# Homes of a kernel's work tiles set by a list, and a hidden unit's six products in a new order

## The chip, the cores and the metric

The kernel runs on one core of a Trainium2 chip. The metric is device time in microseconds of one execution, median of three runs: 706.25 us before (706.14 to 706.48).

## The reference

Attention through 32 memory slots per head, followed by a two-layer network with ELU, all float32:

```
a      = softmax of phi over the sequence            # phi [8, 8, 576, 32]
k_m    = a^T k ;  v_m = a^T v                        # per image and head [32, 64]
attn   = softmax over slots of (q k_m^T / 8)         # [576, 32]
x      = attn v_m, heads side by side                # [4608, 512]
h      = x w_in                                      # w_in [512, 2048]
g      = h if h > 0 else exp(min(h, 0)) - 1
out    = g w_out                                     # w_out [2048, 512]
```

There are 8 images (b) of 8 heads and 576 tokens.

## The kernel before

**Algebra.** v_m and w_in are multiplied first: for each image and each quarter c of the 2,048 hidden channels, `vw` (L723, matmuls at L557) makes a tile vw of 256 rows (8 heads x 32 slots, as two halves of 128) by 512 channels. Then h of a block is the product of vw with the softmax probabilities A (256 slots by 288 tokens, a half image).

**Two parts.** Products of float32 are split: a value is a high part (rounded to the fp32r type) and a low part (the rest), and a product is high x high + low x high + high x low. ScalarE writes the high part (`vw_high` L735, `probs_high` L701 and L702, `elu_high` L826), VectorE the low one (`vw_low` L741, `probs_low` L716, `elu_low` L832).

**A unit.** `order` lists 256 units (image b, half hf, channel tile j of 128 channels). For each, `hidden` (L770 on, matmuls at L779) issues six matmuls of 128x288 into one PSUM tile psh: three passes by two halves g of the slots. Weights (the stationary operand) are 128 columns of the vw tile, the moving operand is a part of A. Then ScalarE and VectorE make ELU (L794, L795, L806, L814), and `project` (by way of `by_channels`, L840) issues six matmuls of 128x512 for the two whole tiles of 128 tokens: there the weights are columns of gp (the two parts of g) and the moving operand is a row block wout[j] of w_out (two parts). The 32 tokens that remain of each half are gathered in rest tiles and projected together for two images (48 matmuls of L840).

**Order of the work.** Nothing is scheduled automatically: a list written out by hand (`FIRST`) gives the order of all steps of the first images, then a plan with a place for each step goes on. Each engine takes its instructions in that order and waits on semaphores. Hidden units run one to two units ahead of their project. Image 0 and 1 have their own front part; later ones prepare attention within the units of the image before.

**Homes.** SBUF tiles come from two pools, `const` (ident, win0 to win3) and `work`. A tile with a tag takes the next of the tag's `bufs` buffers; tags lie behind one another in the order in which they are first asked for. Tag vw has three buffers (three of four c of an image), the fourth, c = 3 of image 2 on, has a home of its own (tag c3). A has four buffers, gp three. wout0 to wout7 have one home each, wout8 to 11 lie in tag late2, wout12 to 15 in tag late3. The vw tile's four parts (high and low, two halves) lie 2,048 bytes apart, A's four parts 1,152, gp's two parts 1,024, a wout's two parts 2,048. Worked out from the sizes in their order, the homes modulo 512 bytes are:

| tile | before | after |
|---|---|---|
| the three vw homes | 160, 160, 160 | 416, 0, 64 (vw0, vw1, vw2) |
| c3 | 416 | 448 |
| A (all four) | 288 | 416 |
| gp (all three) | 416 | 288 |
| wout0 | 288 | 288 |
| wout1 to wout7 | 416 | 320, 352, 384, 416, 448, 480, 0 |
| wout8 to 11 (late2) | 224 | 0 |
| wout12 to 15 (late3) | 416 | 448 |

The queries of image 0 (qh) lie in the output buffers (tag osb); four touches, small DMAs at the start on ScalarE's queue, have small tiles of their own.

Of the kernel before, what the change touches and what calls it, by code (L numbers as in the profile page):

```python
# [1 line left out]

# [6 lines left out]
F32 = mybir.dt.float32  # L9
# [7 lines left out]
P = 128  # L17
# [20 lines left out]

W_SCALE = 2.0**-112
PASSES = ((HI, HI), (LO, HI), (HI, LO))  # L40


def rows_of(c):
# [126 lines left out]
"""  # L170


@with_exitstack
def fused_kernel(ctx: ExitStack, tc: tile.TileContext, phiT, phi, phit, kv0, kvt, kv, q0, q1, w_in, w_out, out):

# [14 lines left out]
    dram = ctx.enter_context(tc.tile_pool(name="dram", bufs=2, space=bass.MemoryType.DRAM))  # L190

    ident = const.tile([P, P], F32, name="ident")
    const.tile([P, 8], F32, name="pad_ident")
    make_identity(nc, ident)

    win = [const.tile([P, NPAIR, CW], F32, name=f"win{c}") for c in range(NVC)]
# [3 lines left out]

    spare = [work.tile([P, 4 * CW], F32, name="spare", tag="vw", bufs=NVB) for _ in range(2)]
    SPARE = {"e0": 0, "e1": 512, "e2": 1024, "x0": 1536, "x1": 1664, "k0": 1792,
             "sc0": 2048, "sc1": 2624, "pr0": 3200, "pr1": 3264}

# [47 lines left out]


    def load_phi(b):
        t = work.tile([P, 2, S], F32, name="ph", bufs=1)
        if b == 0:
            for g in range(2):
                nc.sync.dma_start(t[:, g], phiT[b, :, g])  # L260
        else:
            nc.sync.dma_start(t, phiT[b])
        st[b]["ph"] = t
# [13 lines left out]
    def spread_max(b):  # L277

        s = st[b]
        d = dram.tile([P, 2], F32, name="nmd")  # L280
        nc.sync.dma_start(d, s["nm"])
        s["nmb"] = work.tile([P, P, 2], F32, name="nmb", bufs=1)
        nc.sync.dma_start(
            s["nmb"].rearrange("p x a -> p (x a)"),
            d.rearrange("x a -> (x a)").partition_broadcast(P),
        )
# [63 lines left out]

    def load_half_q(b, hf):
        if b == 0:
            t = work.tile([P, NPAIR, HALF], F32, name="qh", tag="osb", bufs=2)
        else:
            t = half_of_1(hf).rearrange("p (a n) -> p a n", a=NPAIR)
        t0 = hf * HALF
        nc.sync.dma_start(t, q0[b, :, hf])
        for u, (u0, u1) in enumerate(units(b)):
            if t0 <= u0 < t0 + HALF:
                st[b]["q"][u] = t[:, :, u0 - t0 : u1 - t0]  # L360
# [67 lines left out]
    def dec_high(k):  # L428

        i = tiles[k][1]  # L430
        late = dict(tag=f"late{i // 4}", bufs=4) if i >= 8 else dict(bufs=1)
        wout[i] = work.tile([P, 2, DM], F32R, name=f"wout{i}", **late)
        nc.scalar.copy(wout[i][:, HI, :], made(k).rearrange("p r n -> p (r n)"))

# [9 lines left out]
    def phi_max(b, g=None):  # L444
        s = st[b]
        if "nm" not in s:
            s["nm"] = work.tile([P, 2], F32, name="nm")
            s["sums"] = work.tile([P, 2], F32, name="sums")
        g = slice(0, 2) if g is None else slice(g, g + 1)
        eng = nc.gpsimd if b in max_on_pool else nc.vector  # L450
        eng.tensor_reduce(s["nm"][:, g], s["ph"][:, g], AX.X, ALU.max, negate=True)
# [8 lines left out]
    def slot_scale(b):  # L460
        s = st[b]
        sums = s["sums"]
        nc.vector.tensor_scalar(sums, sums, EPS, None, ALU.add)
        rinv = work.tile([P, 2], F32, name="rinv")
        nc.vector.reciprocal(rinv, sums)
        s["rinv"] = rinv

# [61 lines left out]
    def kv_copy(b, i=(0, 1)):  # L529
        s = st[b]  # L530
        if "kvm" not in s:
            s["kvm"] = work.tile([P, 2, P], F32, name="kvm", bufs=2)
        ps = s["ps"].pop(("kv", i))
        if b >= NB:
            nc.scalar.copy(s["kvm"][:, i[0] : i[-1] + 1], ps)
            return
        if 0 in i:
            keys = s["keys"]
            for a in range(2):
                r = slice(64 * a, 64 * a + 64)  # L540
                copy = nc.vector.tensor_copy if (b, a) in keys_on_dve else nc.scalar.copy
                copy(keys[r, :, a * M : (a + 1) * M], ps[r, 0].rearrange("p (j m) -> p j m", m=M))
        if 1 in i:
            nc.scalar.copy(s["kvm"][:, 1], ps[:, len(i) - 1])
# [64 lines left out]
        s["sc"][u] = sc.rearrange("p (n m) -> p n m", m=SQ)  # L609

    def softmax_max(b, u):
        mx = work.tile([P, 2 * HALF // SQ], F32, name="mx")
        if b < NB:
            for ps, g in zip(st[b]["ps"]["s", u], TOKENS):
                nc.vector.tensor_reduce(
                    mx[:, g], ps.rearrange("p (n m) -> p n m", m=SQ), AX.X, ALU.max
                )
        else:
            sc = st[b]["sc"][u]
            mx = mx[:, : sc.shape[1]]  # L620
            nc.vector.tensor_reduce(mx, sc, AX.X, ALU.max)
        st[b]["mx", u] = mx
# [25 lines left out]
    def softmax_sum(b, u):  # L648
        sc = st[b]["sc"][u]
        n = sc.shape[1]  # L650
        sm = work.tile([P, 2 * HALF // SQ], F32, name="sm")[:, :n]
        nc.vector.tensor_reduce(sm, sc, AX.X, ALU.add)
        nc.vector.tensor_scalar(sm, sm, EPS, None, ALU.add)
        rs = work.tile([P, 2 * HALF // SQ], F32, name="rs")[:, :n]
        nc.vector.reciprocal(rs, sm)
        st[b]["rs", u] = rs

# [39 lines left out]
    def probs_high(b, u):  # L697
        s = st[b]
        if b < NB:
            A = s["A"][u] = work.tile([P, 2, 2, HALF], F32R, name="A", bufs=4)  # L700
            nc.scalar.copy(A[:, HI, :, : NT * P], s["ps"]["p", u])  # L701
            nc.scalar.copy(A[:, HI, :, NT * P :], s["pr", u])  # L702
            return
        for hf, src, dst in probs_parts(b, u):
            if s["A"][hf] is None:
                s["A"][hf] = work.tile([P, 2, 2, HALF], F32R, name="A", bufs=4)
            nc.scalar.copy(s["A"][hf][:, HI, :, dst], s["pr", u][:, :, src])

    def probs_low(b, u):
# [19 lines left out]
    def vw_high(b, c, n0=0, n1=CW, parts=(0, 1)):  # L729
        s = st[b]  # L730
        if s["vw"][c] is None:
            home = dict(tag="c3", bufs=1) if b >= NB and c == NVC - 1 else dict(tag="vw", bufs=NVB)
            s["vw"][c] = work.tile([P, 2, 2, CW], F32R, name="vw", **home)
        for a in parts:
            nc.scalar.copy(s["vw"][c][:, HI, a, n0:n1], s["ps"]["vw", c, n0][a])  # L735

    def vw_low(b, c, n0=0, n1=CW, parts=(0, 1)):
        s = st[b]
        t = s["vw"][c]
        for a in parts:  # L740
            nc.vector.tensor_tensor(  # L741
                t[:, LO, a, n0:n1], s["ps"]["vw", c, n0][a], t[:, HI, a, n0:n1], ALU.subtract
            )

    blocks = [(0, 0, 4), (1, 0, 4), (0, 4, 8), (1, 4, 12), (0, 8, 16), (1, 12, 16)]
# [17 lines left out]
    def rest_of(b, j):  # L763

        p, i = b // 2, j // 8
        if (p, i) not in rests:
            rests[p, i] = work.tile([P, 8, P], F32, name="rest", bufs=2)
        return rests[p, i][:, j % 8, :]

    def hidden(it):  # L770
        b, hf, j = order[it]
        s = st[b]
        t = s["vw"][j // 4]
        c0 = (j % 4) * P
        ps = ps_h.tile([P, HALF], F32, name="psh")
        n = 0
        for x, y in PASSES:
            for g in range(2):
                nc.tensor.matmul(  # L779
                    ps,  # L780
                    t[:, x, g, c0 : c0 + P],
                    s["A"][hf][:, y, g, :],
                    start=(n == 0),
                    stop=(n == 5),
                )
                n += 1
        gs[it] = ps

    def elu_exp(it):
        ps = gs[it]
        gf = work.tile([P, HALF], F32, name="gf", bufs=5)
        nc.scalar.activation(gf, ps, AF.Relu, scale=-1.0)  # L794
        nc.scalar.activation(gf, gf, AF.Exp, scale=-1.0)  # L795
        gs[it] = gf, ps
# [25 lines left out]
        nc.gpsimd.tensor_copy(rest_of(b, j)[:, o : o + REST], gf[:, NT * P :])  # L822

    def elu_high(it):
        gp = work.tile([P, 2, NT * P], F32R, name="gp", bufs=3)
        nc.scalar.copy(gp[:, HI], gs[it][:, : NT * P])  # L826
        gs[it] = gs[it], gp

# [51 lines left out]

    def rest_high(p, i):
        gf = rests[p, i // 4][:, i % 4 * 2 : i % 4 * 2 + 2, :]
        gp = work.tile([P, 2, NT * P], F32R, name="gp", bufs=3)
        nc.scalar.copy(gp[:, HI], gf.rearrange("p j n -> p (j n)"))  # L884
        gs["rest", p, i] = gf, gp

# [21 lines left out]
                out[2 * p + n // 2, n % 2, NT * P :], t[n * REST : (n + 1) * REST, :]  # L908
            )

    tiny = work.tile([P, 1], F32, name="tiny", bufs=1)
    work.tile([P, 24], F32, name="pad_tiny", bufs=1)
    warm = ps_o.tile([P, P], F32, name="pso00")

    touched = {
# [5 lines left out]
        "out": w_out[0][:, :8],  # L921
    }

    def touch(x):
        rows = touched[x]
        n = 16 * list(touched).index(x)
        t = work.tile([P, 16], F32, name=f"touch{n}", bufs=1)
        if x in ("in", "out"):
            t, rows = t.bitcast(U32), rows.bitcast(U32)
        nc.scalar.dma_start(t, rows)  # L930
# [168 lines left out]
```

## Time and profile before

| what | value |
|---|---|
| median of three runs | 706.25 us |
| the profiled execution | 706.02 us |
| its span, first to last instruction | 704.2 us |
| TensorE matmuls, busy | 695.2 us, 99% of the span |
| VectorE, ScalarE, busy | 454.7 us, 455.8 us |
| GpSimd, busy | 69.2 us |
| DMA | 64.50 MB in 26,450 packets |

A matmul's busy time runs from its start to the end of its drain, so busy times of matmuls that follow one another overlap, and the mean of one is longer than the distance of two starts. That distance has to be read from starts in order of time. A row of the order in time merges neighbouring instructions of a line: its start, its length to the last one's end, and the count.

### The profile page before, as it was taken

The page shows a single profiled execution, that of the slowest core. Times are in us where ns is not written, and L with a number is a line of the kernel's source. Part 1 is how long each engine was busy: PE and PEld are TensorE (multiplying, and loading weights), DVE is VectorE, ACT ScalarE, POOL GpSimd, SP SyncE. Part 2 cuts the span into 40 slices and gives each one's busy share as a digit, 9 for nine tenths or more (in the row PEclk, how much of TensorE's full clock was granted, in tenths as well). Part 3 has the DMA queues.
Part 4 walks back from the last instruction along what each step waited for, and adds up shares of the span by engine and source line. Part 5 has one row for each costly group of instructions (what it writes and reads, how often), then busy time and mean ns, then how long its engine had stood idle before and what let it go on. Part 6 is the DMA issues. An engine that isn't in the chain of part 4 may idle for free.

```text
span 704.2 us, 13637 instructions
## 1 busy us (share of the span) xinstructions
PE 695.2 (99%) x5112; PEld 579.1 (82%) x5112; DVE 454.7 (65%) x1207; ACT 455.8 (65%) x1101; POOL 69.2 (10%) x117
## 2 busy tenths in 40 slices
PE   8999999999999999999999999999999999999997
PEld 7778787878878888888887888878888888788886
DVE  4989887976686459554864648764683636944442
ACT  3879988877457556575654746765574655756652
POOL 0332342123000200020000200010000010000000
PEclk9999999999999999999999999999999999999999
DMA  8982023351313400351003520243001430000001
GB/s 339 407 356 90 1 63 121 114 153 24 135 39 110 175 31 2 98 172 69 1 1 112 165 76 1 65 118 126 31 1 52 119 152 31 1 31 1 30 2 46
DMA packets 26450, 64.50 MB, mean 92 GB/s; under 512 B 3984, under 2 KB 8592, under 8 KB 26384
## 3 DMA queue, kind: packets, MB, share of 16 engines
q1 hardware_dynamic: 25712, 63.46, 26.4%
q8 instruction: 41, 0.67, 0.4%
q10 hardware_dynamic: 672, 0.16, 0.1%
q14 instruction: 25, 0.20, 0.1%
HBM read 54.17 MB, written 9.44 MB: 90 GB/s over the span
## 4 chain that ended last, share of the span: by engine, by line
PE 94%; DMA 4%; DVE 0%; ACT 0%; issue 0%; SPq 0%
PE pso L840 57%; PE psh L779 29%; PE psb L557 4%; PE psb L498 2%; PE pso L557 2%; DMA raw<-w_out 2%; DMA raw<-w_in 1%; DMA qh<-q 1%; DMA touch<-kv 0%; PE psb L526 0%; PE psb L570 0%; PE pso L570 0%; PE psh L673 0%; SPq L323 0%; DVE A L716 0%
## 5 line engine op out<-in xcount | busy, mean ns | idle before, releaser
L840 PE MATMUL pso<-wout,gp 128*128 128x512 f32 x1728 | 439.2, 394 | 0.0
L840 PEld LDWEIGHTS pso<-wout,gp 128*128 128x128 f32 x1728 | 310.1, 188 | 61.3 <-issue 2.1
L779 PEld LDWEIGHTS psh<-A,vw 128*128 128x128 f32 x1536 | 226.6, 188 | 33.4 <-issue 9.2
L779 PE MATMUL psh<-A,vw 128*128 128x288 f32 x1536 | 244.0, 296 | 0.6 <-ACT A L702 0.4
L794 ACT ACTIVATE gf<-psh 128x288 f32<-128x288 f32 x256 | 105.1, 411 | 101.3 <-PE psh L779 98.1
L806 DVE SCALAR_TENSOR_TENSOR gf<-gf,psh 128x256 f32<-128x256 f32 x192 | 80.7, 420 | 136.4 <-ACT gf L795 135.8
L826 ACT CAST gp<-gf 128x256 fp32r<-128x256 f32 x256 | 103.2, 404 | 78.5 <-DVE gf L806 66.7
L832 DVE TENSOR_TENSOR gp<-gf,gp 128x256 fp32r<-128x256 f32 x256 | 113.4, 446 | 50.7 <-ACT gp L826 49.9
L795 ACT ACTIVATE gf<-gf 128x288 f32<-128x288 f32 x256 | 113.9, 445 | 8.1
L299 POOL TENSOR_TENSOR e<-e,nmb 128x512 f32<-128x512 f32 x12 | 16.4, 1384 | 359.4 <-ACT gf L794 234.7
L803 DVE SCALAR_TENSOR_TENSOR gf<-gf,psh 128x288 f32<-128x288 f32 x64 | 28.5, 450 | 17.5 <-ACT gf L795 15.8
L814 DVE SCALAR_TENSOR_TENSOR rest<-gf,psh 128x32 f32<-128x32 f32 x192 | 34.6, 180 | 0.0
L741 DVE TENSOR_TENSOR vw<-psb,vw 128x512 fp32r<-128x512 f32 (+2 forms) x48 | 26.9, 583 | 4.4 <-ACT vw L735 4.4
L884 ACT CAST gp<-rest 128x256 fp32r<-128x256 f32 x32 | 12.6, 405 | 21.9 <-PE pso L840 21.9
L822 POOL COPY rest<-gf 128x32 f32<-128x32 f32 x64 | 18.7, 319 | 70.3 <-DVE gf L803 62.8
L889 DVE TENSOR_TENSOR gp<-rest,gp 128x256 fp32r<-128x256 f32 x32 | 12.9, 420 | 15.7 <-ACT gp L884 15.6
L735 ACT CAST vw<-psb 128x512 fp32r<-128x512 f32 (+2 forms) x48 | 22.5, 496 | 0.4 <-PE psb L557 0.4
L557 PE MATMUL psb<-win,kvm 64*32 64x512 f32 (+2 forms) x384 | 22.3, 521 | 0.0
L397 ACT ACTIVATE mag<-raw 128x512 uint32<-128x512 uint32 x30 | 20.0, 671 | 2.7 <-DVE win L419 1.4
L393 ACT ACTIVATE mag<-raw 128x512 f32<-128x512 f32 x30 | 19.7, 667 | 1.0 <-DMA raw<-w_in 0.8
L741 DVE TENSOR_TENSOR vw<-pso,vw 128x512 fp32r<-128x512 f32 (+1 forms) x28 | 17.2, 625 | 0.7 <-ACT vw L735 0.6
L937 PE MATMUL pso<-ident 128*128 128x128 f32 x84 | 13.4, 325 | 1.6 <-POOL ident masks.py:199 1.6
(134 smaller groups left out, 445.8 us busy)
## 6 DMA issues: line engine op xcount, KB each, us to landing
kvt<-kv SPq DMA_DIRECT2D x32, 512.0 KB, 7.3
raw<-w_in SPq DMA_DIRECT2D x15, 512.0 KB, 9.7
raw<-w_out SPq DMA_DIRECT2D x15, 512.0 KB, 8.8
out<-osb SPq DMA_DIRECT2D x14, 512.0 KB, 2.8
qt<-q SPq DMA_DIRECT2D x18, 384.0 KB, 3.8
ph<-phiT SPq DMA_DIRECT2D x7, 576.0 KB, 5.1
e<-phi SPq DMA_DIRECT2D x12, 256.0 KB, 5.1
kvt<-kvt SPq DMA_DIRECT2D x8, 256.0 KB, 7.9
```

The source lines that it names most:

```text
L557: nc.tensor.matmul(outs[a][32 * j : 32 * j + 32, :], lhs[r, 32 * j : 32 * j + 32], rhs[r, j], start=True, stop=True, tile_position=(64 * a ...
L735: nc.scalar.copy(s["vw"][c][:, HI, a, n0:n1], s["ps"]["vw", c, n0][a])
L741: nc.vector.tensor_tensor(t[:, LO, a, n0:n1], s["ps"]["vw", c, n0][a], t[:, HI, a, n0:n1], ALU.subtract)
L779: nc.tensor.matmul(ps, t[:, x, g, c0 : c0 + P], s["A"][hf][:, y, g, :], start=(n == 0), stop=(n == 5),)
L794: nc.scalar.activation(gf, ps, AF.Relu, scale=-1.0)
L795: nc.scalar.activation(gf, gf, AF.Exp, scale=-1.0)
L803: nc.vector.scalar_tensor_tensor(gf, gf, -1.0, ps, ALU.add, ALU.max)
L806: nc.vector.scalar_tensor_tensor(gf[:, :n], gf[:, :n], -1.0, ps[:, :n], ALU.add, ALU.max)
L814: nc.vector.scalar_tensor_tensor(rest_of(b, j)[:, o : o + REST], gf[:, n:], -1.0, ps[:, n:], ALU.add, ALU.max)
L826: nc.scalar.copy(gp[:, HI], gs[it][:, : NT * P])
L832: eng.tensor_tensor(gp[:, LO], gf[:, : NT * P], gp[:, HI], ALU.subtract)
L840: nc.tensor.matmul(ps, gp[:, y], wout[j][:, x, :], start=(first and n == 0), stop=(last and n == 2),)
```

## The change

All work tiles get their homes by a list, `LAYOUT`, that is asked for at the start in that order (with fillers of 32 and 64 bytes); tiles then name their tags. The tile vw has parts 2,176 bytes apart in the order high 0, high 1, low 1, low 0. The three vw homes are named one by one and taken in a cycle. From unit 8 on, `hidden` issues its six products in the order TURN: for half 0 low x high, high x high, high x low, then the same for half 1 (weights' part first); units 0 to 7 keep the order of before (PLAIN). The queries of image 0 take buffers of tag A, the touches lie in one buffer of tag gf. Instructions keep their counts and shapes.

```diff
+PIECE = {(HI, 0): 0, (HI, 1): 1, (LO, 1): 2, (LO, 0): 3}
+STEP = CW + 32
+TURN = ((LO, 0, HI), (HI, 0, HI), (HI, 0, LO), (LO, 1, HI), (HI, 1, HI), (HI, 1, LO))
+PLAIN = ((HI, 0, HI), (HI, 1, HI), (LO, 0, HI), (LO, 1, HI), (HI, 0, LO), (HI, 1, LO))
+def piece(t, x, a, n0, n1):
+    o = PIECE[x, a] * STEP
+    return t[:, o + n0 : o + n1]
+SMALL = [("tiny", 32, 1)] + [(t, 8, 2) for t in ("nm", "sums", "rinv")]
+SMALL += [(t, 72, 2) for t in ("mx", "sm", "rs")]
+LAYOUT = SMALL + [("A", 4608, 4), ("vw0", 8576, 1), ("gp", 2048, 3), ("wout0", 4096, 1)]
+for i in range(1, 8):
+    LAYOUT += [(None, 32, 1), (f"wout{i}", 4096, 1)]
+LAYOUT += [("vw1", 8576, 1), ("gf", 1152, 5), ("late2", 4096, 4), ("t4k", 4096, 6), ("osb", 4096, 2)]
+LAYOUT += [("t2k", 2048, 7), ("kvm", 1024, 2), (None, 64, 1), ("vw2", 8576, 1), ("c3", 9216, 1)]
+LAYOUT += [("late3", 4096, 4), ("rest", 4096, 2), ("nmb", 1024, 1), ("ph", 4608, 1)]
...
-    const.tile([P, 8], F32, name="pad_ident")
...
-    spare = [work.tile([P, 4 * CW], F32, name="spare", tag="vw", bufs=NVB) for _ in range(2)]
+    homes(work)
+    spare = [work.tile([P, 4 * CW], F32, name="spare", tag=f"vw{i}", bufs=1) for i in range(2)]
+    vw_homes = itertools.cycle(("vw2", "vw0", "vw1"))
...
-            t = work.tile([P, NPAIR, HALF], F32, name="qh", tag="osb", bufs=2)
+            t = work.tile([P, NPAIR, HALF], F32, name="qh", tag="A", bufs=4)
...
-            home = dict(tag="c3", bufs=1) if b >= NB and c == NVC - 1 else dict(tag="vw", bufs=NVB)
-            s["vw"][c] = work.tile([P, 2, 2, CW], F32R, name="vw", **home)
+            home = "c3" if b >= NB and c == NVC - 1 else next(vw_homes)
+            s["vw"][c] = work.tile([P, 4 * STEP - 32], F32R, name="vw", tag=home, bufs=1)
         for a in parts:
-            nc.scalar.copy(s["vw"][c][:, HI, a, n0:n1], s["ps"]["vw", c, n0][a])
+            nc.scalar.copy(piece(s["vw"][c], HI, a, n0, n1), s["ps"]["vw", c, n0][a])
...
-        n = 0
-        for x, y in PASSES:
-            for g in range(2):
-                nc.tensor.matmul(
-                    ps,
-                    t[:, x, g, c0 : c0 + P],
-                    s["A"][hf][:, y, g, :],
-                    start=(n == 0),
-                    stop=(n == 5),
-                )
-                n += 1
+        for n, (x, g, y) in enumerate(PLAIN if it < 8 else TURN):
+            nc.tensor.matmul(
+                ps, piece(t, x, g, c0, c0 + P), s["A"][hf][:, y, g, :], start=(n == 0), stop=(n == 5)
+            )
...
-    work.tile([P, 24], F32, name="pad_tiny", bufs=1)
...
-        t = work.tile([P, 16], F32, name=f"touch{n}", bufs=1)
+        if not spots:
+            spots.append(work.tile([P, HALF], F32, name="gf", tag="gf", bufs=5))
+        t = spots[0][:, n : n + 16]
```

## Rows read from the trace of the kernel before

**Rows 1.** The spans and the granted clock.
```profile
core 0: 704.2 us, clock 1.000
```
**Rows 2.** The page, busy us, share of the span and instructions.
```profile
PE 695.2 (99%) x5112; PEld 579.1 (82%) x5112; DVE 454.7 (65%) x1207; ACT 455.8 (65%) x1101; POOL 69.2 (10%) x117
```
**Rows 3.** Busy time by stretch: stretch, its length, then us and instructions by engine.
```profile
220.00:640.00 420.00, 420.00 (x3035) 350.40 (x3034) 256.47 (x742) 260.94 (x638) 18.38 (x20) 1.00 0.21 70
```
**Rows 4.** TensorE's waits: us in total, times, longest us.
```profile
PE pso L937 <- POOL ident masks.py:199: 1.6, 1, 1.6
PE psh L779 <- ACT A L702: 0.4, 1, 0.4
```
**Rows 5.** Groups of TensorE's matmuls by form: busy us, mean ns, idle before.
```profile
L840 PE MATMUL pso<-wout,gp 128*128 128x512 f32 x1728 | 439.2, 394 | 0.0
L779 PE MATMUL psh<-A,vw 128*128 128x288 f32 x1536 | 244.0, 296 | 0.6 <-ACT A L702 0.4
```
**Rows 6.** TensorE in order of time, 552 to 570: start us, length us, count.
```profile
552.25 0.95 PE L779 MATMUL psh<-A,vw 128*128 128x288 f32 x6
554.42 0.95 PE L779 MATMUL psh<-A,vw 128*128 128x288 f32 x6
...
558.77 0.95 PE L779 MATMUL psh<-A,vw 128*128 128x288 f32 x6
560.94 0.95 PE L779 MATMUL psh<-A,vw 128*128 128x288 f32 x6
563.12 0.96 PE L779 MATMUL psh<-A,vw 128*128 128x288 f32 x6
565.30 0.94 PE L779 MATMUL psh<-A,vw 128*128 128x288 f32 x6
567.46 0.94 PE L779 MATMUL psh<-A,vw 128*128 128x288 f32 x6
569.61 0.55 PE L779 MATMUL psh<-A,vw 128*128 128x288 f32 x3
```
**Rows 7.** The same view, a stretch from 188.92 without hidden units.
```profile
188.69 4.47 PE L840 MATMUL pso<-wout,gp 128*128 128x512 f32 x19
```
**Rows 8.** The same view, the slowest undisturbed pair, from 118.73.
```profile
118.73 0.96 PE L779 MATMUL psh<-A,vw 128*128 128x288 f32 x6
119.53 1.55 PE L840 MATMUL pso<-wout,gp 128*128 128x512 f32 x6
120.92 1.74 PE L779 MATMUL psh<-A,vw 128*128 128x288 f32 x12
```
**Rows 9.** Groups of weight loads by form.
```profile
L840 PEld LDWEIGHTS pso<-wout,gp 128*128 128x128 f32 x1728 | 310.1, 188 | 61.3 <-issue 2.1 <-ACT gf L795 1.9 <-ACT gp L826 1.7
L779 PEld LDWEIGHTS psh<-A,vw 128*128 128x128 f32 x1536 | 226.6, 188 | 33.4 <-issue 9.2 <-DVE gp L832 2.5 <-DVE gf L803 1.6
```
**Rows 10.** Low parts of A: order of time from 57 on, and who waited.
```profile
58.87 1.79 PE L779 MATMUL psh<-A,vw 128*128 128x288 f32 x12
58.46 0.69 DVE L716 TENSOR_TENSOR A<-psh,A 128x512 fp32r<-128x512 f32 x1 [0.65 <-ACT A L701]
59.07 0.22 DVE L716 TENSOR_TENSOR A<-win,A 128x64 fp32r<-128x64 f32 x1
PEld psh L779 <- DVE A L716: 0.6, 2, 0.3
```
**Rows 11.** The touches and the first gf: ns min/median/max, first and last start us.
```profile
L930 ACTq DMA_DIRECT2D touch<-q x1: 454/454/454, 2.2 to 2.2; - x1
DMA to landing us min/median/max: 3.2/3.8/5.4
L794 ACT ACTIVATE gf<-psh x256: 391/412/441, 24.3 to 685.3; 128x288 f32<-128x288 f32 x128
```
**Rows 12.** Readers of image 0's queries, and writers of A, likewise.
```profile
L570 PE MATMUL pso<-spare,qh x32: 217/275/294, 12.7 to 24.2; 128*128 128x64 f32 x32
L701 ACT CAST A<-psh x2: 572/580/587, 52.1 to 57.9; 128x512 fp32r<-128x512 f32 x2
```
**Rows 13.** The group of products with kvm as weights that costs most.
```profile
L557 PE MATMUL psb<-win,kvm 64*32 64x512 f32 x256 | 17.4, 601 | 0.0
```
**Rows 14.** DMA issues of w_out's raw tiles: count, KB, us to landing.
```profile
raw<-w_out SPq DMA_DIRECT2D x15, 512.0 KB, 8.8
```

More of the change, by code (lines that the diff above doesn't have):

```diff
@@ L1 @@
+import itertools
 from contextlib import ExitStack
@@ L170, with homes, home, pad @@
 """
+def homes(work):
+    n = 0
+    def home(tag, size, bufs=1):
+        work.tile([P, size // 4], F32, name=f"home_{tag}", tag=tag, bufs=bufs)
+    def pad(size):
+        nonlocal n
+        n += 1
+        home(f"pad{n}", size)
+    for tag, size, bufs in LAYOUT:
+        if tag:
+            home(tag, size, bufs)
+        else:
+            pad(size)
 @with_exitstack
@@ L256, in load_phi @@
     def load_phi(b):
-        t = work.tile([P, 2, S], F32, name="ph", bufs=1)
+        t = work.tile([P, 2, S], F32, name="ph", tag="ph", bufs=1)
         if b == 0:
@@ L281, in spread_max @@
         nc.sync.dma_start(d, s["nm"])
-        s["nmb"] = work.tile([P, P, 2], F32, name="nmb", bufs=1)
+        s["nmb"] = work.tile([P, P, 2], F32, name="nmb", tag="nmb", bufs=1)
         nc.sync.dma_start(
@@ L430, in dec_high @@
         i = tiles[k][1]
-        late = dict(tag=f"late{i // 4}", bufs=4) if i >= 8 else dict(bufs=1)
+        late = dict(tag=f"late{i // 4}", bufs=4) if i >= 8 else dict(tag=f"wout{i}", bufs=1)
         wout[i] = work.tile([P, 2, DM], F32R, name=f"wout{i}", **late)
@@ L446, in phi_max @@
         if "nm" not in s:
-            s["nm"] = work.tile([P, 2], F32, name="nm")
-            s["sums"] = work.tile([P, 2], F32, name="sums")
+            s["nm"] = work.tile([P, 2], F32, name="nm", tag="nm", bufs=2)
+            s["sums"] = work.tile([P, 2], F32, name="sums", tag="sums", bufs=2)
         g = slice(0, 2) if g is None else slice(g, g + 1)
@@ L463, in slot_scale @@
         nc.vector.tensor_scalar(sums, sums, EPS, None, ALU.add)
-        rinv = work.tile([P, 2], F32, name="rinv")
+        rinv = work.tile([P, 2], F32, name="rinv", tag="rinv", bufs=2)
         nc.vector.reciprocal(rinv, sums)
@@ L531, in kv_copy @@
         if "kvm" not in s:
-            s["kvm"] = work.tile([P, 2, P], F32, name="kvm", bufs=2)
+            s["kvm"] = work.tile([P, 2, P], F32, name="kvm", tag="kvm", bufs=2)
         ps = s["ps"].pop(("kv", i))
@@ L611, in softmax_max @@
     def softmax_max(b, u):
-        mx = work.tile([P, 2 * HALF // SQ], F32, name="mx")
+        mx = work.tile([P, 2 * HALF // SQ], F32, name="mx", tag="mx", bufs=2)
         if b < NB:
@@ L650, in softmax_sum @@
         n = sc.shape[1]
-        sm = work.tile([P, 2 * HALF // SQ], F32, name="sm")[:, :n]
+        sm = work.tile([P, 2 * HALF // SQ], F32, name="sm", tag="sm", bufs=2)[:, :n]
         nc.vector.tensor_reduce(sm, sc, AX.X, ALU.add)
         nc.vector.tensor_scalar(sm, sm, EPS, None, ALU.add)
-        rs = work.tile([P, 2 * HALF // SQ], F32, name="rs")[:, :n]
+        rs = work.tile([P, 2 * HALF // SQ], F32, name="rs", tag="rs", bufs=2)[:, :n]
         nc.vector.reciprocal(rs, sm)
@@ L699, in probs_high @@
         if b < NB:
-            A = s["A"][u] = work.tile([P, 2, 2, HALF], F32R, name="A", bufs=4)
+            A = s["A"][u] = work.tile([P, 2, 2, HALF], F32R, name="A", tag="A", bufs=4)
             nc.scalar.copy(A[:, HI, :, : NT * P], s["ps"]["p", u])
@@ L705, in probs_high @@
             if s["A"][hf] is None:
-                s["A"][hf] = work.tile([P, 2, 2, HALF], F32R, name="A", bufs=4)
+                s["A"][hf] = work.tile([P, 2, 2, HALF], F32R, name="A", tag="A", bufs=4)
             nc.scalar.copy(s["A"][hf][:, HI, :, dst], s["pr", u][:, :, src])
@@ L741, in vw_low @@
             nc.vector.tensor_tensor(
-                t[:, LO, a, n0:n1], s["ps"]["vw", c, n0][a], t[:, HI, a, n0:n1], ALU.subtract
+                piece(t, LO, a, n0, n1), s["ps"]["vw", c, n0][a], piece(t, HI, a, n0, n1), ALU.subtract
             )
@@ L766, in rest_of @@
         if (p, i) not in rests:
-            rests[p, i] = work.tile([P, 8, P], F32, name="rest", bufs=2)
+            rests[p, i] = work.tile([P, 8, P], F32, name="rest", tag="rest", bufs=2)
         return rests[p, i][:, j % 8, :]
@@ L792, in elu_exp @@
         ps = gs[it]
-        gf = work.tile([P, HALF], F32, name="gf", bufs=5)
+        gf = work.tile([P, HALF], F32, name="gf", tag="gf", bufs=5)
         nc.scalar.activation(gf, ps, AF.Relu, scale=-1.0)
@@ L824, in elu_high @@
     def elu_high(it):
-        gp = work.tile([P, 2, NT * P], F32R, name="gp", bufs=3)
+        gp = work.tile([P, 2, NT * P], F32R, name="gp", tag="gp", bufs=3)
         nc.scalar.copy(gp[:, HI], gs[it][:, : NT * P])
@@ L882, in rest_high @@
         gf = rests[p, i // 4][:, i % 4 * 2 : i % 4 * 2 + 2, :]
-        gp = work.tile([P, 2, NT * P], F32R, name="gp", bufs=3)
+        gp = work.tile([P, 2, NT * P], F32R, name="gp", tag="gp", bufs=3)
         nc.scalar.copy(gp[:, HI], gf.rearrange("p j n -> p (j n)"))
@@ L909, in rest_store @@
             )
-    tiny = work.tile([P, 1], F32, name="tiny", bufs=1)
-    work.tile([P, 24], F32, name="pad_tiny", bufs=1)
+    tiny = work.tile([P, 1], F32, name="tiny", tag="tiny", bufs=1)
     warm = ps_o.tile([P, P], F32, name="pso00")
@@ L922, in fused_kernel @@
     }
+    spots = []
     def touch(x):
```

## The prediction

> **What bounds the kernel now.** I read the views in this order: the spans, the page's busy shares, the busy time by stretch, the waits, the groups by line, then TensorE's matmuls in order of time. [...] The profiled execution took 706.02 us, 1.8 us beyond its span and 0.2 below the median of the three runs (706.25); sums below are made against 706.02 and shifted by 0.2 at the end. TensorE is busy for 695.2 of 704.2 us [rows 2], and from 220 to 640 us for all of 420.00, while VectorE and ScalarE are busy for 256 and 261 [rows 3]. TensorE's own waits are single events of 1.6 and 0.4 us [rows 4]. So the end is set by how fast matmuls follow one another, not by what they wait for. Two lines carry it: L840 (the output products, 1728 of 128x512) and L779 (the hidden products, 1536 of 128x288) [rows 5]. A unit is six of L779 and six of L840 are its two channel tiles; I call the twelve a pair, and there are 256.
>
> Now the pace. Eight pairs in a row run from 552.25 to 569.61: 17.36 us, 2.170 each [rows 6]. But not all alike: the first seven starts are 2.17 or 2.18 apart, the last two pairs (565.30, 567.46, 569.61) take 2.155. The instructions, shapes and order are identical; what differs is the homes they read: hidden products of those two read the vw tile in c3's home, the others one of the three vw homes. Within the unit the same shows: six L779 in a vw home span 0.95 or 0.96, in c3's home 0.94 [rows 6]. Without its last matmul (0.29, [rows 5] has 296 ns) that is 0.130 a slot against 0.132 to 0.134. The fastest project slots stand in a stretch without hidden units: 19 in 4.47 us, less the last one's 0.39, is 0.2267 each [rows 7]. All-best pair: 6 x 0.130 + 6 x 0.2267 = 2.140. The slowest undisturbed pair that I found takes 2.19 (118.73 to 120.92) [rows 8]. The spread that homes could explain, by these rows, is thus 2.14 to 2.19.
>
> **The change part by part.** *Homes and the 2,176 byte step.* While matmul n streams its moving operand, the weights of n+1 are read. I take the distance of the two starts (weights of n+1 less moving of n, modulo 512 bytes, the pattern that the homes of before make) as what the change moves. Before, a hidden unit in a vw home goes through 384, 256, 384, 256, 128 and leaves at 256; in c3's home 128, 0, 128, 0, 384, leaving at 256. The new step of 2,176 (128 modulo 512, as the 1,152 of A's parts) with the new order makes it one constant in a unit: 0 in vw0, 96 in vw1, 160 in vw2, 32 in c3, leaving at 0. In project it was 0 for wout1 to 7 and 12 to 15, 128 for wout0, 192 for wout8 to 11; it becomes -32i for wout0 to 7, and 288 and 352 for the late ones. Distance 0 is in the 0.130 mean of c3's units and in the 0.2267 of [rows 7], and the dearest slots are in units that pass 256 and 384.
>
> The trace of before has no pair with the new distances, so this is bounded from both sides by the ends above. Best: 2.140 everywhere, (2.170 - 2.140) x 256 = 7.7 us less. Worst: 2.19 everywhere, 0.020 x 256 = 5.1 us more. I take the pair that is nearest in kind, c3's at 2.155, whose hidden distances stay mostly low: 0.015 x 256 = 3.8 us less. Its project distance is 192, so a distance other than 0 in project is not by itself dear; that is why I don't charge -32i.
>
> [...]
>
> *The order of six products.* LDWEIGHTS are as many as matmuls in both lines (1728, 1536) [rows 9], though L840 uses each half of gp twice in a row, so repeating weights in the new order saves no load: nothing. But A's low part is now needed by the third product instead of the fifth (2 x 0.130 = 0.26 us earlier), and the low weights by the first. Units 0 to 7 keep the old order. From unit 8 on, the one place where it bites is 58.87: two units start there while VectorE makes A's low part until 59.29 (59.07 + 0.22) [rows 10]. The old order needs it at 58.87 + 0.52 = 59.39, in time; the new at 59.13, 0.16 late. Weights are waited for nowhere (A's parts are the only DVE product of these that the loads wait for, 0.6 us in two [rows 10]). I charge 0.2 us; if vw's low half were late as well at each of the later images, some 0.26 x 6 = 1.6.
>
> *Touches in a gf buffer, queries in A's buffers.* The touches are issued by 2.2 us and land in at most 5.4; the first gf is written at 24.3 [rows 11], so the cover is 16 us: nothing. Were it gone, ScalarE would wait before one activation, with nothing of TensorE's behind it for a unit. The queries of image 0 are last read at 24.2 us, and the A tiles that now follow them in the same buffers are written from 52.1 on [rows 12]: nothing. If it were late, hidden unit 8 would be.
>
> *The rest.* Homes of kvm, the win tiles and the raw tiles move too. The products by kvm are short in total (256 of 128 x 512 kind in 17.4 us, the dearest group [rows 13]); at the same 1% either way that is 0.2 us, taken as 0. VectorE and ScalarE have a third of their time free [rows 3]. DMAs keep sizes and order; the early chain hangs on raw tiles that land in 8.8 us [rows 14], and nothing in the trace prices their new start addresses: 0, bounds a tenth of one load either way, 0.9 us.
>
> **Sum.** 706.0 - 3.8 + 0.2 = 702.4 against the profiled execution, 702.5 rounded with the shift of 0.2 against the median. What is late next is unchanged: TensorE's next slot.
>
> **The rivals.**
> *Homes make no difference, or the gains and losses cancel* (706.2). [...] Against: the steady 0.015 to 0.03 between pairs that differ in homes alone.
> *Slower.* [...] If 0 is what makes the 0.2267 slots and any other distance costs, pairs go to the slowest row, 2.19: 706.2 + 5.1 = 711.3. It decides from where the mean pair is above 2.170, that is, when project loses more than the 0.015 which hidden can win. For it: the only row at 0.2267 has distance 0 [rows 7]. Against: the two best pairs have 192.
> [...]
>
> **How the numbers follow.** Forecast 0.57, no difference 0.18, slower 0.20, much larger gain 0.05. The forecast's own range is 698 (all pairs at 2.140) to 704.5. Within 0.2% means within 1.4 us of 706.25, about what a measurement can tell from no change; a little of the forecast's case falls in it too. So faster 0.60, same 0.20, slower 0.20. The range 697 to 710.5 leaves out most of the larger gain, the tip of the forecast's case, and the upper half of the slower one.
>
> **What would show it.** Right: x6 rows of L779 at 0.94 in every home, pair starts 2.155 or less apart, L840's slots no slower than now in stretches without hidden units; counts and ScalarE's and VectorE's durations unchanged. Wrong: pairs that change by wout (slow at -128 to -224, or in the late eight) would show that project's distance counts; all pairs at 2.17 as now, that homes don't; a TensorE wait on A's low part after 60 us, that the order costs more than one place.

## The result, and the profile after

The changed kernel takes 711.17 us (median of four runs, 710.51 to 711.84), against 706.25 for the kernel before, measured beside it (706.14 to 706.48). The ratio is 1.0069, with a 95% interval of 1.0052 to 1.0087: slower by 0.7%. The forecast was 702.5 with a range up to 710.5, so it has the wrong sign, and the time lies outside the range. The profiled execution took 710.51 us, against 706.02.

The page and the spans of the kernel after: the span, the busy line (us, share of the span, instructions), and the granted clock.

```profile
core 0: 708.7 us, clock 0.999
PE 699.8 (99%) x5112; PEld 580.9 (82%) x5112; DVE 455.9 (64%) x1207; ACT 456.7 (64%) x1101; POOL 69.7 (10%) x117
```

The span grows by 4.5 us [rows 1] and TensorE's busy time by 4.6 [rows 2], with every count as before. VectorE, ScalarE and GpSimd move by 1.2 us or less, the weight loads by 1.8. Here are the groups of TensorE's matmuls by form in the kernel after; its L874, L818 and L598 are the L840, L779 and L557 of before.

```profile
L874 PE MATMUL pso<-wout,gp 128*128 128x512 f32 x1728 | 442.8, 396 | 0.0
L818 PE MATMUL psh<-A,vw 128*128 128x288 f32 x1536 | 245.4, 297 | 0.9 <-DVE A L757 0.4 <-ACT A L743 0.4
L598 PE MATMUL psb<-win,kvm 64*32 64x512 f32 x256 | 17.4, 601 | 0.0
```

The project products carry +3.6 us and the hidden ones +1.4 [rows 5], which is the whole difference within the overlap of busy times (a project matmul's is 396 ns long, and the next one starts 0.233 us after it started); the products by kvm stand still [rows 13]. The same stretch of 420 us as in [rows 3], in the kernel after:

```profile
220.00:640.00 420.00, 420.00 (x3018) 348.85 (x3017) 256.17 (x736) 259.35 (x634) 18.47 (x20) 1.00 0.22 70
```

TensorE is again busy throughout at a granted clock of 1.00, but issues 3018 matmuls instead of 3035. It has not begun to wait; each slot is a little longer. The order of time shows by how much (start us, length us, count):

```profile
555.48 0.95 PE L818 MATMUL psh<-A,vw 128*128 128x288 f32 x6
...
557.67 0.95 PE L818 MATMUL psh<-A,vw 128*128 128x288 f32 x6
...
570.79 0.96 PE L818 MATMUL psh<-A,vw 128*128 128x288 f32 x6
...
572.99 0.43 PE L818 MATMUL psh<-A,vw 128*128 128x288 f32 x2
```

From 555.48 to 572.99 stand eight pairs: 17.51 us, 2.189 each, where before had 2.170 [rows 6], and the quick pairs of 2.155 are gone. 0.019 x 256 pairs is 4.9 us, the whole of the result. Split by starts, over all units and groups that no wait and no other product interrupts, the six hidden slots of a pair went from 788.1 to 793.6 ns and a group of three project slots, of which a pair has two, from 690.6 to 697.8: (5.5 + 2 x 7.2) x 256 = 5.1 us.

### The profile page after: what moved, and what is told of

Its sections match the earlier page's. It is cut to its first block, busy times and chain, and to the rows that moved or that the text cites. A ratio compares the mean times of both kernels' runs of the same rounds, so it can differ in the third digit from the quotient of the medians.

```text
span 708.7 us, 13639 instructions
## 1 busy us (share of the span) xinstructions
PE 699.8 (99%) x5112; PEld 580.9 (82%) x5112; DVE 455.9 (64%) x1207; ACT 456.7 (64%) x1101; POOL 69.7 (10%) x117
## 4 chain that ended last, share of the span: by engine, by line
PE 97%; ACT 1%; DVE 1%; issue 0%; POOL 0%; POOLq 0%
PE pso L874 57%; PE psh L818 29%; PE psb L598 4%; PE psb L539 2%; PE pso L598 2%; PE pso L974 1%; PE pso L611 1%; PE psb L567 0%; PE pso L539 0%; PE psb L611 0%; PE psh L539 0%; ACT mag L434 0%; ACT gf L829 0%; ACT mag L438 0%; ACT gf L828 0%
## 5 line engine op out<-in xcount | busy, mean ns | idle before, releaser
L874 PE MATMUL pso<-wout,gp 128*128 128x512 f32 x1728 | 442.8, 396 | 0.0
L874 PEld LDWEIGHTS pso<-wout,gp 128*128 128x128 f32 x1728 | 310.8, 188 | 62.7 <-issue 2.1
L818 PEld LDWEIGHTS psh<-A,vw 128*128 128x128 f32 x1536 | 227.6, 188 | 35.1 <-issue 9.2
L818 PE MATMUL psh<-A,vw 128*128 128x288 f32 x1536 | 245.4, 297 | 0.9 <-DVE A L757 0.4
L840 DVE SCALAR_TENSOR_TENSOR gf<-gf,psh 128x256 f32<-128x256 f32 x192 | 80.6, 420 | 138.2 <-ACT gf L829 137.3
L866 DVE TENSOR_TENSOR gp<-gf,gp 128x256 fp32r<-128x256 f32 x256 | 115.7, 454 | 51.1 <-ACT gp L860 50.3
L598 PE MATMUL psb<-win,kvm 64*32 64x512 f32 (+2 forms) x384 | 22.3, 521 | 0.0
```

The lines of the kernel that those rows point to most:

```text
L598: nc.tensor.matmul(outs[a][32 * j : 32 * j + 32, :], lhs[r, 32 * j : 32 * j + 32], rhs[r, j], start=True, stop=True, tile_position=(64 * a ...
L818: nc.tensor.matmul(ps, piece(t, x, g, c0, c0 + P), s["A"][hf][:, y, g, :], start=(n == 0), stop=(n == 5))
L840: nc.vector.scalar_tensor_tensor(gf[:, :n], gf[:, :n], -1.0, ps[:, :n], ALU.add, ALU.max)
L866: eng.tensor_tensor(gp[:, LO], gf[:, : NT * P], gp[:, HI], ALU.subtract)
L874: nc.tensor.matmul(ps, gp[:, y], wout[j][:, x, :], start=(first and n == 0), stop=(last and n == 2),)
```

## The experiments

A *distance* below is the start of the weights less that of the moving operand, as in the prediction. Where only the list of homes is edited, the diff gives its core. The kernel before, run beside them, had medians of 706.12, 706.27 and 706.19 us in the three sets of timed runs.

**TensorE alone, one distance at a time.** Two tiles in fixed places, blocks of 24 matmuls of one kind, nothing else on the chip's engines. Stores of the output by DMA run beside the first blocks, to about 35 us by an estimate: 9.4 MB take 25 us at the 378 GB/s that the kernel before moved in its first 40 us, counted from the first matmul at 9.3.

```diff
+for d in range(0, 128, 8):   # project: weights d words further on
+    u = [(d + y * 256 + t * P, x * 512) for t in range(2) for x, y in PASSES]
+    block(f"proj{4 * d}x", u * 4, 512)
...                           # plain: hidden, old order and step; turn: the new ones
```

> Leaves out the whole computation: TensorE alone, 16 blocks of 24 matmuls per pattern, every block at one distance (weights' home less moving home modulo 512 bytes, 0 to 480 in steps of 32), the other engines idle. Distance theory: the project pattern runs at 0.2267 us a slot at distance 0 and at 0.229 to 0.2345 elsewhere, so that a block (23 slots and a drain) takes 5.60 us at 0 and 5.66 to 5.78 elsewhere; the old hidden pattern is shorter at 128 (home of c3 before, 0.130) than at 384 (vw homes before, 0.1315); the new hidden pattern has nothing below 0.130, and 32 as its worst. Rival (distance doesn't matter, the differences come from other engines' traffic or from what ran before): all blocks of a pattern equal within 0.02 us.

The order of time of that run (start us, length us; the number in the name is the distance in bytes):

```profile
19.96 5.61 PE L38 MATMUL proj0x<-mov,wei 128*128 128x512 f32 x24
25.41 5.75 PE L38 MATMUL proj32x<-mov,wei 128*128 128x512 f32 x24
31.00 5.76 PE L38 MATMUL proj64x<-mov,wei 128*128 128x512 f32 x24
...
53.41 5.67 PE L38 MATMUL proj192x<-mov,wei 128*128 128x512 f32 x24
58.92 5.76 PE L38 MATMUL proj224x<-mov,wei 128*128 128x512 f32 x24
64.51 5.61 PE L38 MATMUL proj256x<-mov,wei 128*128 128x512 f32 x24
69.96 5.75 PE L38 MATMUL proj288x<-mov,wei 128*128 128x512 f32 x24
...
121.81 3.35 PE L38 MATMUL plain128x<-mov,wei 128*128 128x288 f32 x24
...
147.31 3.35 PE L38 MATMUL plain384x<-mov,wei 128*128 128x288 f32 x24
...
160.07 3.31 PE L38 MATMUL turn0x<-mov,wei 128*128 128x288 f32 x24
...
169.57 3.39 PE L38 MATMUL turn96x<-mov,wei 128*128 128x288 f32 x24
```

Starts of neighbouring blocks, divided by 24, give the slot: 0.227 us at distance 0 (25.41 - 19.96 = 5.45) and the same again at 256, 0.230 at 192 (5.51), 0.233 at 32, 64, 224 and the rest (5.59 to 5.61). So homes matter with every other engine idle, the pattern repeats after 256 bytes, and in project 0 is best, 192 second, and everything else dear by nearly 3%. The stores play no part: distance 0 beside them and 256 after them take the same 5.45 us. The expectation for hidden missed: 128 and 384, which I took for c3's home against a vw home, are equal to the last digit. In the new order hidden's slots spread wider, from 0.131 at distance 0 to 0.135 at 96 (3.15 and 3.23 us to the next block, over 24), and 96 is where the change puts vw1; the worst was expected at 32.

**The list with the residues of before.** All edits of the change but its homes, step and order.

```diff
-PIECE = {(HI, 0): 0, (HI, 1): 1, (LO, 1): 2, (LO, 0): 3}
-STEP = CW + 32
+PIECE = {(HI, 0): 0, (HI, 1): 1, (LO, 0): 2, (LO, 1): 3}
+STEP = CW
-LAYOUT = ...
+LAYOUT = ...   # modulo 512: vw 160, c3 416, A 288, gp 416, wout0 288, wout1 to 7 416, late2 224, late3 416
-        for n, (x, g, y) in enumerate(PLAIN if it < 8 else TURN):
+        for n, (x, g, y) in enumerate(PLAIN if it < 999 else TURN):
```

> The kernel after with every distance as before (residues of the homes, 2,048 byte step, old order), but homes by a list, queries in A's buffers and touches in a gf buffer. If distances and order carry the 4.9 us: 706.2, within 1. If one of the other edits or the absolute places of the homes carries it: 710 to 711.

706.09 us (705.84 to 707.13), ratio 1.000 (0.9991 to 1.001). Groups by form of this kernel:

```profile
L873 PE MATMUL pso<-wout,gp 128*128 128x512 f32 x1728 | 439.3, 394 | 0.0
L817 PE MATMUL psh<-A,vw 128*128 128x288 f32 x1536 | 244.0, 296 | 0.6 <-ACT A L742 0.4
```

Both lines are back at [rows 5]. The list itself, the queries in A's buffers, the touches in a gf buffer and the cycle of named vw homes cost nothing, and with the residues of before the new places of the tiles make no difference.

**Project back at distance 0.** The change, with all wouts at gp's residue.

```diff
-LAYOUT = SMALL + [("A", 4608, 4), ("vw0", 8576, 1), ("gp", 2048, 3), ("wout0", 4096, 1)]
-for i in range(1, 8):
-    LAYOUT += [(None, 32, 1), (f"wout{i}", 4096, 1)]
+LAYOUT = SMALL + [("A", 4608, 4), ("vw0", 8576, 1), ("gp", 2048, 3)] + [(f"wout{i}", 4096, 1) for i in range(8)]
...   # late2, late3 at the same residue
```

> The kernel after with all 16 wouts at gp's residue 288, so that project's distance is 0 throughout; hidden units as after (order, step, distances 0, 96, 160, 32). Theory that project's distance carries most: project units fall from 697 to 690 ns or less, 576 x 7 = 4.1 us, 707. Rival that the new order or constant hidden distances carry it: 711 with project units still at 695 to 700 because hidden units leave a worse state behind.

708.86 us (708.64 to 709.26), ratio 1.0038 (1.0023 to 1.0053). Groups by form:

```profile
L872 PE MATMUL pso<-wout,gp 128*128 128x512 f32 x1728 | 439.0, 394 | 0.0
L816 PE MATMUL psh<-A,vw 128*128 128x288 f32 x1536 | 246.6, 298 | 0.7 <-ACT A L741 0.4
```

Project returns to the level of before (groups of three at 690.8 ns). But hidden, whose distances this edit leaves alone, got dearer by 1.2 us than in the change: 798.6 ns a unit. That half of the expectation missed. What a hidden slot costs depends on the homes of the project slots beside it too.

**Only project's distances changed.** Hidden as before (its homes, step and order); gp and wouts at the change's distances.

```diff
-STEP = CW + 32
+STEP = CW
+LAYOUT = SMALL + [("gp", 2048, 3), ("wout0", 4096, 1)]
 for i in range(1, 8):
     LAYOUT += [(None, 32, 1), (f"wout{i}", 4096, 1)]
...   # vw, c3 and A as before against each other; PLAIN throughout
```

> Hidden units as before (old order, 2,048 byte step, distances of before), project distances as after (-32i for wout0 to 7, 288, 352 for the late ones). Theory that project's distance carries most: project units at about 697, 710. Rival (order and hidden distances): 706.

710.13 us (710.09 to 710.17), ratio 1.0055 (1.004 to 1.007), as expected. Groups by form:

```profile
L875 PE MATMUL pso<-wout,gp 128*128 128x512 f32 x1728 | 443.3, 397 | 0.0
L819 PE MATMUL psh<-A,vw 128*128 128x288 f32 x1536 | 244.4, 296 | 0.5 <-ACT A L744 0.4
```

Here the pairs differ, modulo 256 bytes, by their wout alone. In order of time, a pair with wout0 (project distance 0) takes 2.17, the next one, with wout1 (-32), 2.19:

```profile
622.71 0.94 PE L819 MATMUL psh<-A,vw 128*128 128x288 f32 x6
...
624.88 0.95 PE L819 MATMUL psh<-A,vw 128*128 128x288 f32 x6
...
627.07 0.95 PE L819 MATMUL psh<-A,vw 128*128 128x288 f32 x6
```

By starts from image 2 on, the mean undisturbed pair is 2.170 with wout0, 2.174 with wout2 (-64, that is 192 modulo 256), and 2.182 to 2.191 with each of the other fourteen. Pairs that change by wout are the sign that the prediction named for project's distance.

Project's distances alone bring 4.0 us (710.13 against 706.12) of the 4.9. The run above with project at 0 has 2.7 from hidden's new distances, with their step and order (708.86 against 706.12); the two parts add to 6.7, not to 4.9, so they are not independent.

**The old order in the changed kernel.**

```diff
-        for n, (x, g, y) in enumerate(PLAIN if it < 8 else TURN):
+        for n, (x, g, y) in enumerate(PLAIN if it < 999 else TURN):
```

> The kernel after with the old order of six products in every unit, homes and the 2,176 byte step kept (hidden distances then change within a unit: by 128, 256, 256, 384, 384 from those of after). Theory that the order itself costs only the wait for A's low part: 710.5 to 711.5, hidden units still at 791 to 797 ns by their homes. Rival (the order carries the hidden part): hidden units back at 788, 709.5.

710.95 us (710.52 to 711.21), ratio 1.0066 (1.0051 to 1.0081): the order is not the cause. Hidden units stand at 795 ns, as expected. 0.2 us is what the wait on A's low part is worth, but it lies within the spread of these runs.

**Pairs alone, 512 sets of homes.** TensorE alone again, now whole pairs: vw, gp and wout in 64-byte steps against A, four pairs of each set, in the old order with the old step, and in a second run with the new ones.

```diff
+for v, g, w in ...:          # each 0 to 448 bytes
+    hidden = [(v + STEP[x, g_], (2 * y + g_) * 288) for x, g_, y in ORDER]
+    project = [(2560 + g + y * 256 + t * P, 2048 + w + x * 512) for t in range(2) for x, y in PASSES]
+    for _ in range(4):
+        unit(ph, hidden, 288)
+        unit(po, project, 512)
```

> Leaves out the whole computation: TensorE alone, four pairs (six hidden, six project products) in a row for each of 512 sets of homes (vw, gp and wout each at 0, 64, ... 448 bytes from A's residue), old order and 2,048 byte step. Distance theory: a pair's time is fixed by the three homes alone and repeats what the kernel shows for the same homes: vw 128, gp 128, wout 448 (the image quarter with 2.155) 2.153 us a pair; vw 384, gp 128, wout 128 2.173. Rival (other engines' traffic or the unit before set it): these two equal, or a spread under 0.01 us over the sets.

> The same with the new order and the 2,176 byte step. Theory that constant hidden distances are no gain: the best set is not below the best of the old order (2.14 to 2.15), and sets with project at 0 or 256 are 0.02 to 0.04 us a pair ahead of those at other distances. Rival (the new order is sound and only the homes were badly chosen): the best set is below 2.14.

The order of time in the first (the names give vw, gp and wout in bytes from A):

```profile
1339.28 0.95 PE L36 MATMUL hv128g128w448x<-mov,wei 128*128 128x288 f32 x6
...
1341.46 0.96 PE L36 MATMUL hv128g128w448x<-mov,wei 128*128 128x288 f32 x6
...
1343.64 0.94 PE L36 MATMUL hv128g128w448x<-mov,wei 128*128 128x288 f32 x6
...
1345.80 0.94 PE L36 MATMUL hv128g128w448x<-mov,wei 128*128 128x288 f32 x6
...
1858.48 0.95 PE L36 MATMUL hv192g128w128x<-mov,wei 128*128 128x288 f32 x6
...
1860.64 0.95 PE L36 MATMUL hv192g128w128x<-mov,wei 128*128 128x288 f32 x6
...
3532.32 0.95 PE L36 MATMUL hv384g128w128x<-mov,wei 128*128 128x288 f32 x6
...
3534.50 0.95 PE L36 MATMUL hv384g128w128x<-mov,wei 128*128 128x288 f32 x6
...
3575.83 0.96 PE L36 MATMUL hv384g128w448x<-mov,wei 128*128 128x288 f32 x6
...
3578.01 0.94 PE L36 MATMUL hv384g128w448x<-mov,wei 128*128 128x288 f32 x6
...
3580.17 0.94 PE L36 MATMUL hv384g128w448x<-mov,wei 128*128 128x288 f32 x6
```

The set of before (384, 128, 128) runs at 2.17 to 2.18, and (128, 128, 128), c3's home, at the same. The set of wouts 8 to 11 beside c3's home (128, 128, 448: project distance 192) takes 2.18 twice and then 2.16 (1343.64 to 1345.80): one set of homes, two paces. The same wouts beside a vw home (384, 128, 448) go through the same two: the second pair takes 2.18 (3575.83 to 3578.01), the third 2.16. So c3's home is not what made the two quick pairs of [rows 6]. The expectation that the homes alone fix a pair's time held from the third pair on, not for the first two. Over all sets the third of the four pairs, the settled one below, lies between 2.153 and 2.214, and by project's distance the means are 2.171 at 0, 2.188 at 64, 2.190 at 128, 2.179 at 192, repeating after 256. (192, 128, 128) is at 2.155 from its second pair on (1858.48 to 1860.64 is 2.16). In the second run the settled pairs lie between 2.155 and 2.200, with means of 2.177 at project distance 0 and 2.178 at 192, 2.184 at 128 and 2.192 at 64: the lead of 0.02 to 0.04 that was expected for 0 is 0.015 at most. Its steady best is 2.16, with vw at A's residue and project at 0:

```profile
257.62 0.94 PE L36 MATMUL hv0g192w192x<-mov,wei 128*128 128x288 f32 x6
...
259.78 0.94 PE L36 MATMUL hv0g192w192x<-mov,wei 128*128 128x288 f32 x6
```

**Three lists picked from these sweeps.** The first with project at 192 (vw and gp at 416 modulo 512, A 288, wouts 224, old order and step). The second with project at 0 and vw and c3 192 above A (A 288, gp and wouts 416, vw and c3 480, old order and step). The third is the change in everything but its list (new order and step; vw and c3 at A's residue modulo 256, gp and wouts 192 above).

```diff
-LAYOUT = ...
+LAYOUT = SMALL + [("gp", 2048, 3)] + [(f"wout{i}", 4096, 1) for i in range(8)] + [("late2", 4096, 4), ("late3", 4096, 4)]
+LAYOUT += [(None, 64, 1)] + [(f"vw{i}", 8192, 1) for i in range(3)] + [("c3", 9216, 1), ("gf", 1152, 5), (None, 192, 1)]
+LAYOUT += [("A", 4608, 4), ("t4k", 4096, 6), ...]   # the second
```

> Old order and step, and everywhere the residues of the two best pairs of before: vw and gp 416, A 288, all wouts 224. Distance theory: all undisturbed pairs at 2.153 as in those two, (2.170 - 2.153) x 256 = 4.4 us less than before, 701.8. Rival (those pairs were quick for their place in the image or in memory): 706, pairs as before by channel tile.

The first missed: 706.29 us (705.72 to 706.78), ratio 1.000 (0.9991 to 1.001). Its order of time shows why; the homes in the two stretches are the same:

```profile
426.02 0.94 PE L816 MATMUL psh<-A,vw 128*128 128x288 f32 x6
...
428.18 0.94 PE L816 MATMUL psh<-A,vw 128*128 128x288 f32 x6
...
441.12 0.95 PE L816 MATMUL psh<-A,vw 128*128 128x288 f32 x6
...
443.30 0.95 PE L816 MATMUL psh<-A,vw 128*128 128x288 f32 x6
```

Pairs run at 2.16 (426.02 to 428.18), then products that make a vw tile come between (from 434.77), and after them pairs run at 2.18 (441.12 to 443.30). From 629.80 on, 25 pairs in a row stand at 2.18 with nothing between them, where TensorE alone needed two to become quick. That the set has a quick pace was not enough here (706.29 us): the kernel would have had to come into it again, and soon.

> Old order and 2,048 byte step; A 288, gp and all wouts 416 (project distance 0), the vw homes and c3 all at 480, that is 192 from A instead of 128. From TensorE alone, where this set settles at 2.153 us a pair from the second pair on (the homes of before at 2.173): 256 x (2.170 - 2.153) = 4.4 us less than before, 701.9, if the settling survives the waits and attention products between the pairs. Rival (as with the set of project distance 192, the quick state is lost at each disturbance): 704 to 706.

702.75 us (702.42 to 703.12), ratio 0.9951 (0.9939 to 0.9963). Groups by form:

```profile
L872 PE MATMUL pso<-wout,gp 128*128 128x512 f32 x1728 | 436.1, 392 | 0.0
L816 PE MATMUL psh<-A,vw 128*128 128x288 f32 x1536 | 243.5, 295 | 0.7 <-ACT A L741 0.4
```

That is 0.85 us short of the gain expected. Its pairs from image 2 on stand at 2.153, save for some next to an interruption (2.159 to 2.181); where products for a vw tile come between, the second pair behind them is quick again (550.34 to 552.50).

> The kernel after in all but its list: all vw homes and c3 at A's residue (hidden distance 0 throughout), gp and all wouts 192 above it (project distance 0). Order and 2,176 byte step kept. From TensorE alone, 2.160 a pair: (2.189 - 2.160) x 256 = 7.4 us less than after, 703.8. Theory that the homes alone made the change slower: below 706. Rival (the new order or step costs by itself, whatever the homes): 708 or more, as with project alone set right.

703.57 us (703.12 to 705.66), ratio 0.9967 (0.9954 to 0.9979). Groups by form:

```profile
L872 PE MATMUL pso<-wout,gp 128*128 128x512 f32 x1728 | 437.7, 393 | 0.0
L816 PE MATMUL psh<-A,vw 128*128 128x288 f32 x1536 | 242.8, 295 | 0.7 <-ACT A L741 0.4
```

Both beat the kernel before and the change. The third is the decisive one for the change: with its order, its step and all its other edits, another list takes 7.6 us off (711.17 to 703.57). The homes of that list alone made it slower.

**Which distance counts.** TensorE alone: in *next* and *own* the moving start walks, so that the distance to the next weights, or to a matmul's own, stays 0 while the other one is the value in the name; in *both* the two are that value.

```diff
+walk = [s * i % 64 for i in range(25)]
+block(f"next{4 * s}x", [(walk[i - 1] if i else 0, walk[i]) for i in range(24)], 512)
+block(f"own{4 * s}x", [(walk[i], walk[i]) for i in range(24)], 512)
+block(f"both{4 * s}x", [(s, 0)] * 24, 512)
```

> Leaves out the whole computation: TensorE alone, blocks of 24 matmuls of 128x512. In blocks next the moving start walks by s bytes from one matmul to the next and the weights of each lie at the moving start of the one before (distance to the next weights 0, distance to its own weights s); in blocks own the weights lie at their own moving start (own distance 0, distance to the next s); in blocks both all is constant and weights lie s from the moving start. Theory that what counts is the distance between the moving operand that streams and the weights of the next: next 0.2267 a slot (a block 5.61 us) for every s, own like both, 0.2333 (5.76) except at s = 0 and 192. Rival (a matmul's distance to its own weights counts): own 0.2267 throughout, next like both.

```profile
37.25 5.70 PE L38 MATMUL next32x<-mov,wei 128*128 128x512 f32 x24
42.78 5.62 PE L38 MATMUL own32x<-mov,wei 128*128 128x512 f32 x24
48.24 5.76 PE L38 MATMUL both32x<-mov,wei 128*128 128x512 f32 x24
...
120.47 5.75 PE L38 MATMUL next192x<-mov,wei 128*128 128x512 f32 x24
126.06 5.73 PE L38 MATMUL own192x<-mov,wei 128*128 128x512 f32 x24
131.62 5.67 PE L38 MATMUL both192x<-mov,wei 128*128 128x512 f32 x24
```

The trace of before shows that the weights of the next matmul are loaded while one runs. The load for the first hidden product behind a project unit starts with the unit's last matmul and takes 0.19 us, and that product starts at 556.59:

```profile
556.37 0.39 PE L840 MATMUL pso<-wout,gp 128*128 128x512 f32 x1
556.37 0.19 PEld L779 LDWEIGHTS psh<-A,vw 128*128 128x128 f32 x1
```

Neither theory holds. If one distance alone decided, the row of that name, which keeps it at 0, would stand at the 5.60 of distance 0 and the other would equal *both*; at 192 both single ones are dearer (5.75, 5.73) than the two together (5.67). The weights' address by itself is not the rule either: *own32* takes its weights from all eight steps of 32 bytes in turn and stands at 5.62, *both32* from one of them at 5.76. The name in the prediction, distance to the next weights, is at most a part of the rule.

## Why the prediction was wrong

**What held.** TensorE's pace is the bound: it has no new idle time that counts, and the 4.9 us are 256 times 0.019. The other edits are worth nothing, as charged (the list with the residues of before). The order saves no load (5112, as before), and costs the one wait that was charged at 0.2. Here is that place in the kernel after, the two units in order of time and the loads' waits (us in total, times, longest):

```profile
58.46 2.03 PE L818 MATMUL psh<-A,vw 128*128 128x288 f32 x12
PEld psh L818 <- DVE A L757: 1.1, 3, 0.6
```

The two units take 2.03 us instead of 1.79 [rows 10], 0.24 more, and there is no second place of that kind. With the old order in the changed kernel, the waits are back at the 0.6 us of before.

**The step that failed.** "I take the pair that is nearest in kind, c3's at 2.155", with "a distance other than 0 in project is not by itself dear; that is why I don't charge -32i". It had -3.8 us for the homes; the runs give about +4.7 (4.9 less the 0.2 of the order), of which project's distances alone bring 4.0. Two readings in it were wrong.

First, the quick pairs of [rows 6] were put down to c3's home. 128 and 384 are one residue of 256, and both runs of TensorE alone show them equal. Hidden units run two ahead of their project there, so the four pairs from 560.94 to 569.61 read wouts 8 to 11, all at project distance 192: the first two, in a vw home, take 2.18 each, the last two, in c3's home, 2.16 and 2.15. These are the paces, in the same order, that TensorE alone shows for four such pairs with one home throughout. What set the quick pairs apart is thus the quicker of that set's two paces, and [rows 6] itself held two pairs at 192 that were as slow as any. The rows could have warned in another way: vw's and c3's hidden distances, 384, 256, 384, 256, 128 and 128, 0, 128, 0, 384, are the same list modulo 256. I took 512 from the pattern of the homes and did not test a shorter period against the rows.

Second, one other distance was taken to stand for all. 192 is the one good value beside 0 among the steps of 32; the change puts two of the first eight wouts on 0 and 192, and six, with all the late ones, on the dear ones (-32i modulo 256; late2 32, late3 96). By the slots of TensorE alone, each wout weighed alike, that is a mean of 0.2327 instead of 0.2281, 8 us over 1728. Among hidden slots the three-slot groups show 7.2 ns, and 576 of them 4.1 us, since there distance 0 does not reach 0.227 either (690.2 / 3 = 0.230). That is also why pairs of 2.17 with project at distance 0 were no argument against the dearness of the others.

**The rivals.** The slower one is what happened, with its place, its price and its condition: 711.3 forecast, 711.17 measured, pairs at 2.189 where it said 2.19. That the price fits so closely is luck: the pair of [rows 8] reads wout8, at 192 and in its slower pace, and none of the change's dear distances. The two steady pairs at 192, which stood against it, were the exception among the distances. Homes without a difference is out: 703.57 and 711.17 us for the same instructions in the same order, and with every other engine idle the distances make a slot 0.227 or 0.233 us long. The much larger gain, which had a chance of 0.05, rests on no pace that a run shows: in neither sweep of pairs does a pair stay under 2.153, which is 4.4 us below the 2.170 of before over 256 pairs.

**Open.** Why the distances change a slot's length, which no run shows; which distances besides the one to the next weights count; why one set of homes has two paces and what moves it between them. Steps under 64 bytes in whole pairs were not tried.

## What to carry to other kernels

In this kernel, where TensorE is the bound and loads weights for every matmul (5112 of each), the homes of moving operand and weights modulo 256 bytes were worth 0.5% one way (702.75 us) and 0.7% the other (711.17). In one like it, sweep them with TensorE alone before making a list, in the real sequence of products, since neighbours can change each other's price (1.2 us of hidden here, when only project's homes moved). A quick pair in a trace says nothing of its cause until the operand that differs has been varied by itself. Choose a set that comes into its quick pace within a pair or two and measure it in the kernel: of the three lists above, the two that did so gained (702.75 and 703.57 us), and the one that stayed slow behind interruptions did not (706.29).

## What the runs showed of the hardware

Not expected: with TensorE alone and everything else equal, slots of 128x512 products depended on the start addresses (0.227, 0.230 or 0.233 us), with a period of 256 bytes (5.45 us to the next block at 0 and at 256, 5.51 and 5.50 at 192 and 448). Identical pairs in identical homes had two paces (2.153 and 2.18 us). TensorE alone went from the slow to the quick one after two pairs; the kernel with those homes stayed in the slow one for 25. And hidden products changed by 1.2 us in all when only their neighbours' homes moved (245.4 to 246.6).
